# The first unit's gates written out in one fixed order, and its first chunk taken from angles to keys and queries by groups of four heads

## The chip, the cores and the metric

The kernel runs on one core of a Trainium2 chip. The metric is the device time of one execution in microseconds (us). The kernel before took 724.6 us in the median of four runs (722.34 to 727.52).

## The reference, cut to what matters

Two blocks follow each other. The first is a gated linear recurrence over 768 time steps for 4 batches of 8 heads with 48 channels each:

```python
mag = np.sqrt(a_re * a_re + a_im * a_im)
scale = np.minimum(mag, 0.999) / (mag + 1e-06)
a_re_n, a_im_n = (a_re * scale, a_im * scale)
for t in range(S):
    new_re = ar * S_re - ai * S_im          # ar, ai: the gate of step t
    new_im = ar * S_im + ai * S_re
    kv = np.einsum('bhd,bhe->bhde', k[:, :, t], v[:, :, t])
    S_re, S_im = (new_re + kv, new_im)
    y[:, :, t] = np.einsum('bhd,bhde->bhe', q[:, :, t], S_re)
```

The second is a feed-forward block on the 3072 rows of 384 values that come out: `h = x @ w_in` (384 to 2048), `g = h * erf(softplus(h))`, `g @ w_out`. The two weights arrive as 64-bit floats and are narrowed to 32 bits on the chip.

## The kernel before, in words

**The algorithm.** A product of complex gates is the exponential of a sum of logarithms and of a sum of angles. So the recurrence becomes attention in chunks: `g_tan` (L873) makes a_im/a_re from Ln and Exp; `g_mag` (L863) and `g_log` (L883) make the logarithm `lr` of the magnitude; `g_turn` (L891) takes the arctangent; `g_total` (L923) and `g_angle` (L895) sum logarithms and angles along time by a matmul with a triangle; `g_decay` (L927) takes Exp of plus and minus the sum (tile `pr`), and `g_sin` (L915) sine and cosine of the angle (tile `CS`). In `chunk` (L954), `prep` multiplies keys and queries by `pr` (L950, tiles `kr`, `qr`) and by `CS` (L965, tiles `kt`, `qt`); `cols` transposes four heads at a time on TensorE (L973) and copies them out of PSUM (L976); `scores` (L980), `state` (L991) and `xT` (L1010) are the attention itself. `ff_in` (L1043, tile `hps`), `softplus`, `erf_times_h` and `ff_out_7`/`ff_out_8` are the feed-forward block.

**The tiling.** The rows are cut into 12 units of 256 rows, each of two chunks (`c0`, `c1`) of 128. The first matmul of `ff_in` of a unit needs `xT` of both its chunks.

**What sets the order.** The program is traced once, without loops on the chip. A list scheduler then fixes the order on every engine: it goes by the order of tracing and lets an instruction go ahead of earlier ones that, by its own model, are not ready. `in_order` (L710) chains the ScalarE instructions that need a function table, so that tables are not swapped more often than written; `T["hold"]` ties the first VectorE step of a weight's narrowing behind another instruction. The first chunk's gates are traced by hand (L1225 to L1262). All after it is a list `plan` of pairs (time, step), sorted by the numbers in `WHEN` (L47), in which one unit of time is about one unit of rows. `warm` (L1206) issues matmuls whose results nobody reads; each appears as two in the trace.

**Function tables.** Ln and Exp are in one table, Arctan and Sin in a second, Gelu in a third. Every change of table is an `ACT_TABLE_LOAD` on ScalarE (L707).

**Narrowing the weights.** `narrow` (L747) works on 16 pieces of 768 KB: a DMA (`raw`, L763), one ScalarE multiplication (L769) and three VectorE operations (L772, L776, L782).

Of the kernel before, what the change touches and what calls it, by code (L numbers as in the profile page):

```python
# [10 lines left out]
FP = mybir.dt.float32  # L11
# [24 lines left out]
def weave(*streams):  # L36
# [5 lines left out]
    for _, _, _, step in sorted(order, key=lambda e: e[:3]):  # L42
# [4 lines left out]
WHEN = {'qact': 2,  # L47
 'a00': [0.385, 0.377, 0.389, 0.465, 0.427, 0.308, 0.569, 0.485, 0.567, 0.63],
 'a01': [0.526, 0.422, 0.611, 0.633, 0.649, 0.542, 0.659, 0.66, 0.67, 0.681],
 'n': [0.676, 0.782, 0.769, 0.929, 1.105, 1.183, 1.312, 1.472, 1.61, 1.914, 1.96, 2.143, 2.151, 2.632, 2.395],  # L50
 'g1': [0.657, 0.707, 0.747, 0.758, 0.79, 0.797, 0.829],
 'att': {1: [[0.931, 1.297], 1.089], 2: [[1.716, 2.126], 1.029], 3: [[3.038, 3.627], 1.205]},
 'gate': {2: [1.242, 1.289, 1.402, 1.421, 1.453, 1.472, 1.392], 3: [1.516, 1.614, 1.92, 2.114, 2.598, 2.232, 2.18]},
 'hps': {0: [[0.767, 0.876], [1.01, 1.426]],
         1: [[1.788, 2.017], [2.366, 2.708]],
         2: [[3.136, 3.262], [3.538, 3.85]],
         11: [[11.97, 12.305], [12.367, 12.72]]},
 'act': {0: [2.6, 2.924],
         1: [3.335, 3.7],
         2: [4.134, 4.386],  # L60
         3: [4.9, 5.2],
         4: [5.752, 6.098],
         10: [11.679, 12.029],
         11: [12.456, 12.886]},
 'ops': {0: [3.02, 3.377, 3.703],
         1: [4.059, 4.696, 4.846],
         2: [4.454, 4.8, 4.886],
         3: [5.38, 5.6, 6.213],
         10: [12.145, 12.41, 13.01],
         11: [13.169, 13.36, 14.059]},  # L70
 'T': 5.1,
 'gr': [-1.569, -1.419, -1.119, -0.953, -0.478, -0.129, -1.279],
 'st': [0.014, 0.03, 0.059, 0.09, 0.12, 0.15, 0.2, 0.25, 0.28, 0.388],
 'hr': [1.113, 1.509, 1.573, 1.938],
 'ar': [1.565, 1.947],
# [3 lines left out]
 'ag': [5.424, 6.296, 7.239, 8.239, 9.239, 10.239, 11.21],  # L79
# [4 lines left out]
 'qone': 0}  # L84


WARM = (12, 9, 8, 8, 13, 5)
# [511 lines left out]
def quotient_path(  # L599
# [19 lines left out]
    nc = tc.nc  # L619
    B, H, S, D = q.shape  # L620
# [44 lines left out]
    nc.vector.memset(cold, 0.0)  # L665
    ones = const.tile([P, 1], FP, name="ones")
    nc.vector.memset(ones, 1.0)
    half_pi = const.tile([P, 1], FP, name="half_pi")
    nc.vector.memset(half_pi, 0.5 * math.pi)
    turns = const.tile([P, P], FP, name="turns")  # L670
    nc.vector.tensor_scalar(out=turns, in0=triu, scalar1=1.0 / TAU, scalar2=None, op0=OP.mult)
# [3 lines left out]
    for t, x in ((off, 0.0), (large, 0.0), (zeros, 1.0)):  # L675
        nc.vector.memset(t, x)
# [11 lines left out]
    for t in vbuf:  # L688
        nc.vector.memset(t[:, :, :, D:D + GAP], 0.0)
    for t in sbuf:  # L690
        nc.vector.memset(t[:, :, D:D + GAP], 0.0)
# [8 lines left out]
    def act(func, **kw):  # L700
        sets = [nm for nm, fs in TABLES.items() if func in fs]
        if not sets:
            nc.scalar.activation(func=func, **kw)
            return
        if T.get("table") != sets[0]:
            T["table"] = sets[0]
            in_order(nc.scalar.preload_act_table_set(sets[0]))  # L707
        in_order(nc.scalar.activation(func=func, **kw))  # L708
# [38 lines left out]
    def narrow(i, dst, src, home):  # L747
# [6 lines left out]
        def seek(words, i):  # L754
            hi = words.bitcast(FP).rearrange("p (n w) -> p n w", w=2)[:, :, 1]
            nc.vector.tensor_reduce(out=zeros[:, i:i + 1], in_=hi, axis=mybir.AxisListType.X, op=OP.min,  # L756
                                    apply_absolute_value=True)
# [7 lines left out]
        def begin():  # L765
# [3 lines left out]
            ins = nc.scalar.mul(out=lo, in_=lo, mul=2.0**-29)  # L769
            if i < 3:  # L770
                in_order(ins)
            ins = nc.vector.tensor_scalar(out=a, in0=hi, scalar1=0x07FFFFFF, scalar2=3, op0=OP.bitwise_and,  # L772
                                          op1=OP.logical_shift_left)
            if "hold" in T:
                tc.add_manual_dep(ins.ins, T["hold"].ins.name, order, reason="place among others")
            nc.vector.scalar_tensor_tensor(out=a, in0=hi, scalar=0xC0000000, in1=a, op0=OP.bitwise_and,  # L776
                                           op1=OP.bitwise_or)
            T["parts", i] = a, lo

        def end():  # L780
            a, lo = T["parts", i]
            nc.vector.tensor_tensor(out=dst.bitcast(U32), in0=a, in1=lo, op=OP.add)  # L782

        def use():
            begin()
            end()
# [9 lines left out]
        if i < 14:  # L796
            return get, use, again, look, begin, end
# [10 lines left out]
        return get, use, again, look, begin, end  # L808
# [25 lines left out]
    def sums_of_weights(r0, n):  # L834
# [8 lines left out]
        for o, x, y in ((T1, B12, B11), (T2, B22, T1), (T4, B21, T2), (B12, B22, B12)):  # L843
            nc.vector.tensor_tensor(out=o, in0=x, in1=y, op=OP.subtract)
# [18 lines left out]
    def g_mag(u, cc=ALL):  # L863
# [4 lines left out]
        i = u * C + cc[0]  # L868
        act(out=s, in_=ar, func=AF.Square, accum_out=large[:, i:i + 1])
        act(out=y, in_=ai, func=AF.Square)  # L870
        nc.vector.tensor_tensor(out=s, in0=s, in1=y, op=OP.add)

    def g_tan(u, cc=ALL):  # L873
# [4 lines left out]
        nc.vector.tensor_tensor(out=th, in0=th, in1=ai, op=OP.mult)  # L878
        i = u * C + cc[0]
        nc.vector.tensor_reduce(out=off[:, i:i + 1], in_=th, axis=mybir.AxisListType.XY, op=OP.max,  # L880
                                apply_absolute_value=True)

    def g_log(u, cc=ALL):  # L883
# [4 lines left out]
        nc.vector.tensor_scalar(out=s, in0=s, scalar1=0.5, scalar2=math.log(CAP), op0=OP.mult, op1=OP.min)  # L888
        T["logs"] = nc.vector.tensor_tensor(out=g_("lr", u, cc), in0=s, in1=y, op=OP.subtract)
# [5 lines left out]
    def g_angle(u, c):  # L895
# [4 lines left out]
        if goes_on:  # L900
            prev = T["F", u][:, c - 1, :] if c > 0 else T["F", u - 1][:, C - 1, :]
            if not on_pe:
                row = T["s", u][0:1, c, :]
                nc.sync.dma_start(out=row, in_=prev[P - 1:P, :])
                nc.vector.scalar_tensor_tensor(out=th[0:1, :], in0=row, scalar=TAU, in1=th[0:1, :],
# [6 lines left out]
        nc.vector.tensor_scalar(out=F, in0=ps, scalar1=MAGIC, scalar2=MAGIC, op0=OP.add, op1=OP.subtract)  # L912
        nc.vector.tensor_tensor(out=F, in0=ps, in1=F, op=OP.subtract)

    def g_sin(u, cc=ALL):  # L915
# [5 lines left out]
        act(out=CS[:, :, 1, :], in_=F, func=AF.Sin, scale=TAU)  # L921

# [24 lines left out]
    def scaled(nm, e, u, c):  # L947

        a = att1.tile([P, H, D], FP, tag="part", name=nm + "r", bufs=2)
        nc.vector.tensor_tensor(out=a, in0=T[nm, u][:, c], op=OP.mult,  # L950
# [3 lines left out]
    def chunk(u, c):  # L954
# [3 lines left out]
        st = {}  # L958

        def prep(nm, e):  # L960
            def f():
# [3 lines left out]
                T["hold"] = nc.vector.tensor_tensor(out=t, in0=a.unsqueeze(2).to_broadcast([P, H, 2, D]), in1=cs, op=OP.mult)  # L965
# [3 lines left out]
        def cols(nm, g):  # L969
            def f():  # L970
# [5 lines left out]
                (nc.scalar.copy if nm == "k" or u < WHEN["qact"] or g < WHEN["qone"] else nc.vector.tensor_copy)(out=t[0:D2], in_=ps[0:D2])  # L976
# [3 lines left out]
        def scores(g):  # L980
            def f():
# [5 lines left out]
                nc.vector.tensor_tensor(out=A, in0=ps, in1=triu.unsqueeze(1).to_broadcast([P, HG, P]), op=OP.mult)  # L987
# [3 lines left out]
        def state():  # L991
# [10 lines left out]
            else:  # L1002
                t = att1.tile([P, H, D], FP, tag="part", name="Skv", bufs=2)
                for e in range(2):
                    nc.vector.tensor_tensor(out=t[0:D2, e::2, :], in0=kv[0:D2, e::2, :], in1=side(T["S"][0:D2], e), op=OP.add)  # L1005
            for e in range(2):
                nc.vector.tensor_tensor(out=side(ns[0:D2], e), in0=t[0:D2, e::2, :], in1=w[:, e::2, :], op=OP.mult)
            st["S"] = ns

        def xT():  # L1010
# [26 lines left out]
            nc.scalar.copy(out=T["xT", u][:, :, c * P:(c + 1) * P], in_=ps)  # L1037
# [5 lines left out]
    def ff_in(u, sl):  # L1043
        def two(i):
            def f():
# [9 lines left out]
                nc.scalar.copy(out=T["h", u, sl][:, i:i + 2, :], in_=ps)  # L1055
# [15 lines left out]
    def erf_times_h(u, sl):  # L1071
# [3 lines left out]
        def part(i):  # L1075
            def f():
# [4 lines left out]
                nc.vector.tensor_tensor(out=z, in0=z, in1=y, op=OP.mult)  # L1081
                nc.vector.scalar_tensor_tensor(out=y, in0=z, scalar=-2.0, in1=y, op0=OP.add, op1=OP.mult)  # L1082
                nc.vector.tensor_tensor(out=e, in0=e, in1=y, op=OP.mult)  # L1083
                nc.vector.scalar_tensor_tensor(out=h, in0=e, scalar=1.0 / RT2, in1=h, op0=OP.add, op1=OP.mult)  # L1084
# [294 lines left out]
```

## Time and profile before

| | us |
|---|---|
| median of four runs | 724.6 |
| the profiled execution | 721.8 |
| its span, from first to last instruction | 720.0 |
| TensorE busy in the span | 704.0 |
| VectorE busy | 577.2 |
| ScalarE busy | 568.4 |
| 77 table loads on ScalarE, 1.283 us each | 98.8 |
| mean granted TensorE clock, as a share of full speed | 0.998 |

In the lines of the timeline and of the chain the first number is the start in us from the beginning of the span and the second the duration. The chain of waits goes back from the last instruction: each step is followed to what released it, or to the instruction before it on its engine. PE is TensorE's matmuls, PEld its weight loads, DVE VectorE, ACT ScalarE, SP the engine that issues most DMAs. An instruction on ACT or DVE can begin before the one ahead of it has fully ended, so that starts follow each other closer than the durations say.

### The profile page before, as it was taken

To read this page: it belongs to the slowest core of one execution; us is meant where nothing else is said; L and a number is where in the kernel's file an instruction comes from. 1 tells how busy PE (TensorE), PEld (TensorE's weight loads), DVE (VectorE), ACT (ScalarE), POOL (GpSimd) and SP (SyncE) were. 2 spreads that over 40 slices of the span, in tenths; PEclk is the share of its full clock that TensorE was granted. 3 is DMA by queue.
4 is the path that set the end of the run, shared out by engine and by line. 5 is a ranking of instruction groups with operands and counts; after the bars stand their busy time and mean duration, and the time that the engine had idled before them with its cause. 6 is when DMAs were issued, how large, how long until landed. Compare 5 with 4: busy or idle time off the path is not lost.

```text
span 720.0 us, 12616 instructions
## 1 busy us (share of the span) xinstructions
PE 704.0 (98%) x5050; PEld 602.7 (84%) x5050; DVE 577.2 (80%) x1003; ACT 568.4 (79%) x749; POOL 1.1 (0%) x8
## 2 busy tenths in 40 slices
PE   9899999999999999999999999999999999999996
PEld 8778888766777678898998998889898899899985
DVE  5878996777599789979899889797798877876563
ACT  7978949978988998799788688887688487556760
POOL 0000000000000000000000000000000000000000
PEclk9999999999999999999999999999999999999999
DMA  9985784021303211613322423323330400200000
GB/s 215 228 191 120 199 211 94 1 45 34 56 0 57 55 45 25 146 31 76 89 56 55 112 56 68 105 50 67 100 99 23 132 1 23 89 1 23 0 24 27
DMA packets 156012, 54.50 MB, mean 76 GB/s; under 512 B 142612, under 2 KB 145704, under 8 KB 155944
## 3 DMA queue, kind: packets, MB, share of 16 engines
q1 hardware_dynamic: 153864, 53.22, 31.6%
q8 instruction: 41, 0.67, 0.4%
q10 hardware_dynamic: 2080, 0.39, 0.4%
q14 instruction: 27, 0.22, 0.1%
HBM read 48.82 MB, written 4.75 MB: 74 GB/s over the span
## 4 chain that ended last, share of the span: by engine, by line
PE 52%; ACT 24%; DVE 17%; DMA 4%; issue 2%; SPq 0%; ACTq 0%
PE hps L1053 20%; PE ops L1151 14%; ACT z L708 5%; ACT L707 5%; ACT yy L708 4%; PE tr L973 3%; PE y L1033 3%; PE sc L984 3%; DVE z L1081 3%; DVE yy L1082 3%; DVE e L1083 2%; PE kv L996 2%; DVE h L1084 2%; PE ops L1113 2%; DMA again<-in_moe_w_out_dram 2%
## 5 line engine op out<-in xcount | busy, mean ns | idle before, releaser
L1053 PE MATMUL hps<-xT,w_in_sb 128*128 128x256 f32 x1152 | 270.7, 381 | 1.0 <-ACT xT L1037 0.7
L1053 PEld LDWEIGHTS hps<-xT,w_in_sb 128*128 128x128 f32 x1152 | 212.5, 190 | 33.1 <-issue 2.6
L707 ACT ACT_TABLE_LOAD x77 | 98.8, 1283 | 3.3 <-issue 2.1
L1055 ACT COPY h<-hps 128x512 f32<-128x512 f32 x96 | 55.3, 580 | 44.8 <-PE hps L1053 42.1
L708 ACT ACTIVATE e<-z 128x512 f32<-128x512 f32 x96 | 57.3, 626 | 37.1 <-DVE h L1084 36.7
L1081 DVE TENSOR_TENSOR z<-z,yy 128x512 f32<-128x512 f32 x96 | 62.6, 683 | 29.4 <-ACT e L708 28.9
L1113 PE MATMUL ops<-w_out_sb,h 128*128 128x384 f32 x224 | 76.6, 488 | 0.4 <-DVE h L1084 0.4
L1151 PE MATMUL ops<-w_out_sb,h 128*128 128x192 f32 x384 | 70.5, 326 | 0.0
L1151 PEld LDWEIGHTS ops<-w_out_sb,h 128*128 128x128 f32 x384 | 63.6, 190 | 1.4
L1113 PEld LDWEIGHTS ops<-w_out_sb,h 128*128 128x128 f32 x224 | 41.5, 190 | 26.5 <-DVE h L1084 1.2
L1082 DVE SCALAR_TENSOR_TENSOR yy<-z,yy 128x512 f32<-128x512 f32 x96 | 62.4, 682 | 0.1
L1083 DVE TENSOR_TENSOR e<-e,yy 128x512 f32<-128x512 f32 x96 | 62.4, 681 | 0.1
L1084 DVE SCALAR_TENSOR_TENSOR h<-e,h 128x512 f32<-128x512 f32 x96 | 62.4, 680 | 0.1
L708 ACT ACTIVATE z<-h 128x2048 f32<-128x2048 f32 x24 | 45.9, 1913 | 9.7 <-DVE seen L756 4.9
L984 PEld LDWEIGHTS sc<-qT,kT 96*128 96x128 f32 x384 | 47.9, 191 | 5.7 <-DVE qT L976 3.0
L984 PE MATMUL sc<-qT,kT 96*128 96x128 f32 x384 | 50.9, 278 | 1.7 <-DVE qT L976 1.3
L1033 PE MATMUL y<-A,v 128*32 128x128 f32 x768 | 47.6, 278 | 0.6 <-DVE Skv L1005 0.5
L1151 PE MATMUL ops<-T,S 128*128 128x192 f32 x256 | 47.4, 327 | 0.0
L708 ACT ACTIVATE yy<-z 128x2048 f32<-128x2048 f32 x24 | 45.9, 1913 | 0.4
L708 ACT ACTIVATE z<-z 128x2048 f32<-128x2048 f32 x24 | 45.9, 1913 | 0.3
L708 ACT ACTIVATE yy<-yy 128x2048 f32<-128x2048 f32 x24 | 45.9, 1913 | 0.3
L1151 PEld LDWEIGHTS ops<-T,S 128*128 128x128 f32 x256 | 42.3, 190 | 2.1 <-DVE S L1165 0.3
(101 smaller groups left out, 1063.5 us busy)
## 6 DMA issues: line engine op xcount, KB each, us to landing
raw<-in_moe_w_in_dram SPq DMA_DIRECT2D x8, 768.0 KB, 9.4
raw<-in_moe_w_out_dram SPq DMA_DIRECT2D x8, 768.0 KB
again<-in_moe_w_in_dram SPq DMA_DIRECT2D x8, 768.0 KB, 6.3
ar<-in_a_re_dram SPq DMA_DIRECT2D x24, 192.0 KB, 3.1
k<-in_k_dram SPq DMA_DIRECT2D x24, 192.0 KB, 4.1
q<-in_q_dram SPq DMA_DIRECT2D x24, 192.0 KB, 3.6
v<-in_v_dram SPq DMA_DIRECT2D x48, 96.0 KB, 3.3
out_dram<-o SPq DMA_DIRECT2D x24, 192.0 KB, 1.9
```

What stands on the lines that cost most here:

```text
L707: in_order(nc.scalar.preload_act_table_set(sets[0]))
L708: in_order(nc.scalar.activation(func=func, **kw))
L984: nc.tensor.matmul(out=ps[:, j, :], lhsT=st["k", g][0:D2, j, :], rhs=st["q", g][0:D2, j, :], start=True, stop=True)
L1033: nc.tensor.matmul(out=ps[b * QUAD:(b + 1) * QUAD, i, :], lhsT=lhsT, rhs=rhs, start=start, stop=stop)
L1053: nc.tensor.matmul(out=ps[:, e, :], lhsT=w_in_sb[:, kd, f0:f0 + P], rhs=T["xT", u][:, kd, :], start=(kd == 0), stop=(kd == KD - 1))
L1055: nc.scalar.copy(out=T["h", u, sl][:, i:i + 2, :], in_=ps)
L1081: nc.vector.tensor_tensor(out=z, in0=z, in1=y, op=OP.mult)
L1082: nc.vector.scalar_tensor_tensor(out=y, in0=z, scalar=-2.0, in1=y, op0=OP.add, op1=OP.mult)
L1083: nc.vector.tensor_tensor(out=e, in0=e, in1=y, op=OP.mult)
L1084: nc.vector.scalar_tensor_tensor(out=h, in0=e, scalar=1.0 / RT2, in1=h, op0=OP.add, op1=OP.mult)
L1113: nc.tensor.matmul(out=ps, lhsT=lhsT, rhs=w_out_sb[:, i, :], start=i == HALF, stop=i == KF - 1)
L1151: ins = nc.tensor.matmul(out=ps, lhsT=a(sl)[:, i], rhs=b(sl, i), start=sl == 0 and i == 0, stop=sl == NSL - 1 and i == HALF - 1)
```

## The change

**A fixed order.** A class `InOrder` wraps VectorE and ScalarE. While it is on, every instruction is tied behind the one traced before it on its engine. It is on from the first gate instruction of unit 0 to `g_decay(0, 1)`; elsewhere the wrapper does nothing.

**Another order.** Before, both chunks' tangents and magnitudes came first, then the logarithm of c0, Arctan of both, the decay of c0 and the sines of both, and the logarithm of c1 last: the table of Ln and Exp is loaded three times and that of Arctan and Sin twice. Now the logarithm of c0, the tangents of c0 and c1 and the decay of c0 come ahead of the first Arctan, and the magnitude and logarithm of c1 after the last sine: two loads and one. The first step of the narrowing of the first weight piece is split: its VectorE steps (`high`) go ahead of the decay, its ScalarE step and its sum (`low`, `join`) behind all gates.

**By groups.** For chunk 0 of unit 0, `by_heads` does the angle, its sine and cosine and the last multiplication of keys and queries in two halves of four heads, with the absolute value taken on VectorE.

**The rest.** The search for the largest tangent, `g_off`, is a step of its own. The copies of transposed queries out of PSUM go to VectorE for the first chunk and for units from 3 on (before: from 2 on), so that unit 2's are on ScalarE now. `warm` multiplies the zero tile `cold` only, and its counts are others. Many numbers in `WHEN` differ, most by little; unit 1's gates (`g1`) come 0.045 later.

```diff
-WHEN = {'qact': 2,
- 'a00': [0.385, 0.377, 0.389, 0.465, 0.427, 0.308, 0.569, 0.485, 0.567, 0.63],
- 'a01': [0.526, 0.422, 0.611, 0.633, 0.649, 0.542, 0.659, 0.66, 0.67, 0.681],
- 'g1': [0.657, 0.707, 0.747, 0.758, 0.79, 0.797, 0.829],
+WHEN = {'qact': 3,
+ 'a00': [0.385, 0.699, 0.3, 0.32, 0.31, 0.33, 0.569, 0.34, 0.35, 0.63],
+ 'a01': [0.526, 0.422, 0.611, 0.637, 0.649, 0.542, 0.659, 0.66, 0.67, 0.681],
+ 'g1': [0.702, 0.752, 0.792, 0.802, 0.835, 0.842, 0.873],
...
-WARM = (12, 9, 8, 8, 13, 5)
+WARM = (16, 0, 16, 2, 3, 4)
+class InOrder:
+    def __init__(self, tc, engine):
+        self.tc, self.engine, self.on = tc, engine, False
+    def __getattr__(self, name):
+        emit = getattr(self.engine, name)
+        if not self.on:
+            return emit
+        return lambda *args, **kw: self.tc.keep_in_program_order(emit(*args, **kw))
...
+    def by_heads():
+        F = g_("F", 0, (0, 1))[:, 0, :]
+        CS = T["CS", 0] = gat.tile([P, C, 2, DM], FP, tag="CS", name="CS")
+        of = lambda t, g: t[..., g * HG * D:(g + 1) * HG * D]
+        got = {nm: att1.tile([P, H, 2, D], FP, tag=nm + "t", name=nm + "t") for nm in ("k", "q")}
+        def angle(g):
+            ps = ps_a.tile([P, HG * D], FP, tag="a", name="sum")
+            nc.tensor.matmul(out=ps, lhsT=turns, rhs=of(T["th", 0][:, 0, :], g), start=True, stop=True)
+            vector.tensor_scalar(out=of(F, g), in0=ps, scalar1=MAGIC, scalar2=MAGIC, op0=OP.add, op1=OP.subtract)
+            vector.tensor_tensor(out=of(F, g), in0=ps, in1=of(F, g), op=OP.subtract)
+            vector.scalar_tensor_tensor(out=of(CS[:, 0, 0], g), in0=of(F, g), scalar=-1.0, in1=of(F, g), op0=OP.mult, op1=OP.max)
+        def sin(g):
+            act(out=of(CS[:, 0, 1], g), in_=of(F, g), func=AF.Sin, scale=TAU)
+            act(out=of(CS[:, 0, 0], g), in_=of(CS[:, 0, 0], g), func=AF.Sin, scale=-TAU, bias=half_pi)
+        def prep(nm, g):
+            cs = of(CS[:, 0], g).rearrange("p u (h d) -> p h u d", d=D)
+            hh = slice(g * HG, (g + 1) * HG)
+            ins = vector.tensor_tensor(out=got[nm][:, hh], in0=T["r", nm, 0, 0][:, hh].unsqueeze(2).to_broadcast([P, HG, 2, D]),
+                                       in1=cs, op=OP.mult)
+            T["hold"] = ins
+        return angle, sin, prep, got
...
-                (nc.scalar.copy if nm == "k" or u < WHEN["qact"] or g < WHEN["qone"] else nc.vector.tensor_copy)(out=t[0:D2], in_=ps[0:D2])
+                (vector.tensor_copy if nm == "q" and ((u, c) == (0, 0) or u >= WHEN["qact"] and g >= WHEN["qone"]) else scalar.copy)(out=t[0:D2], in_=ps[0:D2])
...
+    angle, sin, prep, T["first"] = by_heads()
     first = chunk(0, 0)
-    for c in range(C):
-        g_tan(0, one[c])
-        g_mag(0, one[c])
-        warm(WARM[1 + c], T["th", 0][:, c])
+    vector.on = scalar.on = True
+    T["table"] = "natural_log_exp_and_others"
+    in_order(scalar.preload_act_table_set(T["table"]))
+    g_mag(0, c0)
     g_log(0, c0)
+    g_tan(0, c0)
+    warm(WARM[1], cold)
+    g_off(0, c0)
     g_total(0, 0)
-    for cc in one:
-        g_turn(0, cc)
-    T["hold"] = T["logs"]
-    wt[0][4]()
-    g_angle(0, 0)
+    g_tan(0, c1)
+    g_off(0, c1)
+    warm(WARM[2], cold)
+    _, _, _, _, high, low, join = wt[0]
+    high()
     g_decay(0, 0)
-    for nm, e in (("k", 1), ("q", 0)):
-        T["r", nm, 0, 0] = scaled(nm, e, 0, 0)
-    wt[0][5]()
+    T["r", "k", 0, 0] = scaled("k", 1, 0, 0)
+    g_turn(0, c0)
+    angle(0)
+    angle(1)
+    warm(WARM[3], cold)
+    g_turn(0, c1)
+    sin(0)
+    prep("k", 0)
+    sin(1)
+    T["r", "q", 0, 0] = scaled("q", 0, 0, 0)
+    prep("k", 1)
+    g_angle(0, 1)
+    warm(WARM[4], cold)
+    prep("q", 0)
+    prep("q", 1)
+    g_mag(0, c1)
+    g_sin(0, c1)
+    g_log(0, c1)
+    g_total(0, 1)
+    g_decay(0, 1)
+    vector.on = scalar.on = False
+    low()
+    join()
     wt[2][0]()
-    warm(WARM[3], T["th", 0][:, 1])
-    g_sin(0, c0)
-    for f in first[:2]:
-        f()
-    g_angle(0, 1)
-    warm(WARM[4], T["th", 0][:, 1])
-    g_sin(0, c1)
     wt[1][1]()
     load_gates(1)
     for j in (3, 4, 5):
         wt[j][0]()
-    g_log(0, c1)
-    g_total(0, 1)
-    g_decay(0, 1)
```

## The prediction

> **What bounds the kernel now.** I read the page's busy times, then windows, the chain of waits and the timeline of the first 55 us.
>
> ```profile
> PE 704.0 (98%) x5050; PEld 602.7 (84%) x5050; DVE 577.2 (80%) x1003; ACT 568.4 (79%) x749; POOL 1.1 (0%) x8
> ```
>
> TensorE is busy for all but 16 us, so the time is its work plus what it loses. Busy isn't useful, though: the groups show 24 + 86 warm matmuls, 5.5 + 10.5 us, all before 22.2. Windows (busy us of PE, PEld, DVE, ACT, POOL, then the granted clock):
>
> ```profile
> 20.00:25.00 5.00, 3.95 (x29) 3.26 (x30) 3.23 (x5) 4.97 (x10) 0.00 (x0) 1.00 0.98 180
> 25.00:30.00 5.00, 4.95 (x50) 4.20 (x49) 4.09 (x7) 5.00 (x15) 0.00 (x0) 1.00 1.02 356
> 60.00:80.00 20.00, 20.00 (x172) 16.70 (x172) 19.61 (x30) 19.29 (x30) 0.00 (x0) 1.00 0.79 193
> 80.00:100.00 20.00, 18.79 (x175) 16.81 (x178) 19.63 (x33) 15.58 (x24) 0.00 (x0) 1.00 0.76 185
> ```
>
> Until 25 ScalarE is the full engine, and TensorE idles or warms. From 25 TensorE is full, so whatever brings useful matmuls forward shortens the end, as long as VectorE, which is full too from 60 to 100, keeps up. The chain (start, duration, what) names ScalarE up to the first scores:
>
> ```profile
> 13.06 1.28 ACT L707
> 14.34 0.01 issue
> 14.35 0.96 ACT pr L708 x3
> ...
> 15.74 1.28 ACT L707
> ...
> 20.38 1.28 ACT L707
> 21.66 0.01 issue
> 21.67 0.52 ACT s L708
> 22.19 0.47 ACT qT L976
> 22.66 0.42 ACT y L708
> 23.09 0.47 ACT kT L976
> 23.56 0.42 ACT y L708
> 23.98 0.48 ACT qT L976
> 24.46 0.04 issue
> 24.51 0.49 PE sc L984 x2
> ```
>
> Keys and queries of c0 are rotated by 19.92 (`qt` starts at 18.97 and takes 0.95), but their copies out of PSUM stand behind a table load and among c1's logarithms: first scores 24.51. Four timeline lines are my milestones: keys of c1, first useful `hps`, keys of unit 1, their transposes.
>
> ```profile
> 29.04 0.94 DVE L965 TENSOR_TENSOR kt<-kr,CS 128x768 f32<-128x768 f32 x1
> ```
> ```profile
> 40.05 3.19 PE L1053 MATMUL hps<-xT,w_in_sb 128*128 128x256 f32 x14
> ```
> ```profile
> 49.59 0.95 DVE L965 TENSOR_TENSOR kt<-kr,CS 128x768 f32<-128x768 f32 x1
> ```
> ```profile
> 53.50 1.04 PE L973 MATMUL tr<-ident,kt 128*96 128x128 f32 x8
> ```
>
> **Step 1: to the decay of c0, in the fixed order.** Rows: 128x384 costs 0.52 on ACT (start to start 0.41, but 0.55 where one reads the last one's result), 0.55 on DVE (0.47). The first Square starts when `ar` lands, 4.53 as now; the second ends at 5.6; DVE adds until 6.16. ACT, which now fills that wait with other work, stands idle 0.6. Ln, Exp, Ln of the magnitude start at 6.19, 6.75, 7.31; `lr` is done at 8.42 (10.65 now). The tangents follow at 7.72, 8.27, 8.69, 9.24. The sum of c0 is on PE from 8.45 to 9.33, so the two Exps of `pr` start at 9.67 behind the tangents and ACT is free at 10.52 (15.20 now). `high` stands ahead of `kr` on DVE and waits for the first weight piece; that was read at 10.57 without a wait, and comes to its turn at 10.93. `kr` is done at 12.93. Moving the weight's ACT step (0.91) and sum (0.96) behind the gates frees that much here; they fall into ACT's and DVE's waits after 22. The DMAs of `wrow` stand in SP's queue behind c1's values, whose issues end at 14.7, so they aren't earlier; unit 1's gate loads, issued from 18.18, now wait for c1's Squares, which end at 16.8: 1.4 us of cover.
>
> **Step 2: angles by halves.** Table load 10.52 to 11.80, Arctan of c0 until 12.33. 32 warm matmuls start behind the sum at 9.10 and take 32 x 0.112 = 3.6, so angle 0 starts at 12.7 and ends at 13.3. DVE has a row for half width, 0.35 (L1172); three dependent steps end at 13.66, 14.04, 14.42, the second half's at 15.46. ACT has no 128x192 row: between 0.26 (half of 0.52) and 0.52, I take 0.36 from the slope between 0.52 at 384 and 0.83 at 768; either end moves nothing, because DVE's order sets the steps after it. Sines of half 0 end at 14.9, of half 1 at 15.95. `prep` of k: 15.93 and 16.87; then `F` of c1 (0.55 twice) until 17.93; q: 18.40 and 18.87. Against 19.92 that is only 1.05 earlier. The two halves cost four extra DVE starts of about 0.15 and the absolute value 2 x 0.35 on DVE instead of 0.52 on ACT, all counted here.
>
> **Step 3: scores of c0.** `kT` is copied by ACT by 18.1, while c1's angle is still on DVE. `qT` goes to DVE (0.68 against 0.58 on ACT), 19.2 to 19.85 and to 20.5. First scores: 19.9, **4.6 earlier**. Here the two dropped table loads count: c1's logarithm no longer stands in the middle.
>
> *Page against row:* the load takes 1.283 and the next ACT instruction starts 0.01 later. The Trainium skill, "ScalarE: Activation LUTs", section "What ACT_TABLE_LOAD costs", adds a drain of about 1.38 to each change of table; by it two loads fewer would save 5.3, by the row 2.57. The measurement decides; no sum here uses 5.3.
>
> **Step 4: keys of c1.** Sines of c1 end at 19.57, table load until 20.85, logarithm until 22.48, `lr` 23.07, sum 24.0, `pr` 24.9; `qt` at 26.1 and `kt` at 27.55, **2.4 earlier** than 29.98.
>
> **Step 5: to the first `hps`.** PE's work from first scores on, by the chain's rows: scores 2 x 1.85, state 2 x 1.32, three sums of 0.65, transposes of c1 4 x 0.44, `y` 1.70 and 2.18, together 13.93. Before, 40.05 - 24.51 = 15.54, so 1.61 was lost. After: until `kt` of c1 PE has 6.40 of work for 7.70 us, 1.30 lost, and the same 1.61 on the copies and masks. First `hps`, with the same work done: 19.9 + 13.93 + 2.91 = 36.74, **3.3 earlier**. Bounds: only the 1.30 lost, 4.9; the copies and masks lose 2 more because narrowing and unit 1's gates come between, 1.3.
>
> **Step 6: the rest.** Unit 2's four `qT` copies leave DVE (4 x 0.68) for ACT (4 x 0.58), between 80 and 110, where DVE is full and PE loses 1.2 from 80 to 100. Worth 0 to 1.2, I take 0.7. The other numbers of `WHEN` shuffle a PE that is full; no row prices them: 0, with 1.5 either way for the range. The start's warm work goes from 110 to 82 instructions, and is worth nothing while the clock stays up. A first-speed warm matmul takes 421 ns against 275 later, the windows show 1.00 until 717 and 0.50 after, and the last matmul ended at 714.46: an idle stretch of 2.5 us is enough. My longest gap is 1.1, before the queries; were the clock lost there, some 3 us of work would take 3 more.
>
> *Page against row:* "TensorE: Matmul & The Clock Gate", Part 1, says that an idle window of about 3.4 us halves the clock, the windows running free of the program, and warns against the gaps that fewer warm matmuls leave. The row's 2.5 is stricter; by neither does 1.1 lose the clock.
>
> **The sum.** The profiled execution took 721.8 (span 720.0, 1.8 around it): 721.8 - 3.3 - 0.7 = 717.8. The median of the runs lies 724.6 / 721.8 = 1.0039 above it: **720.6**. The forecast's own bounds, 1.3 to 6.1 earlier, are 718.5 to 723.3.
>
> **The rivals.**
> A, *the gain is handed back at units 1 and 2.* DVE is 98% busy from 60 to 100 and its work isn't less by more than 2; if it, not PE, sets the pace there, PE meets it again. For: ACT copies of `xT` and DVE's `Skv` hold PE up at 80 to 86. Against: PE loses nothing from 60 to 80. Price: 3.3 of the gain; 724.
>
> B, *slower: unit 1's keys come late.* Its gates stand 0.045 later in the plan, and PE takes the transposes in order. Now `kt` ends at 50.54 for a transpose at 53.50, 3.0 to spare; with `hps` 3.3 earlier, they're due at 50.2. If unit 1's gates slip behind three groups of `ff_in` (12 matmuls, 2.59 each: 7.8), `kt` ends at 58.3, PE stands 8.1, and 4.0 of gain leaves a loss of 4.1: 728.7. It decides once `kt` ends later than 54.2. Against: ACT has 4 us less to do before 40 (two loads, 2.57; one Abs, 0.52; two copies, 1.16), and the scheduler lets ready gates go ahead.
>
> C, *the change doesn't do what it says:* fixed order makes ACT wait (for `F` of c1, for the sum) with c1's logarithm behind it, `kt` of c1 stays near 29.4, and PE makes nothing of early scores: 0.6 earlier, 724.
>
> D, *more:* PE isn't starved for c1 and loses nothing: 19.9 + 13.93 = 33.8, 6.2 earlier, with step 6 some 7: 717.6.
>
> **How the numbers follow.** Forecast 0.60, A 0.17, C 0.08, B 0.09, D 0.06. A measurement can tell about 0.5%, 3.6 us, from no change; that line is 721.0, inside the forecast's own range, and I put 0.42 of its 0.60 below it. Faster: 0.42 + 0.06 = 0.48; same: 0.18 + 0.17 + 0.08 = 0.43; slower: 0.09. The range leaves out B and part of D: 717.5 to 725.0.
>
> **What the profile after would show.** Right: three table loads before 40 us, one of them for Arctan and Sin, instead of five up to 21; first `sc` near 19.9, `kt` of c1 near 27.5, first `hps` near 36.7, transposes of unit 1 near 50. Wrong: an `hps` early and an unchanged end (A), PE idle before unit 1's `tr` (B), `kt` of c1 past 29 (C), or a granted clock of 0.50 before 25.

## The result and the profile after

| | before | after |
|---|---|---|
| median, us (59 and 38 runs) | 723.97 | 725.8 |
| profiled execution / its span, us | 721.8 / 720.0 | 725.2 / 723.5 |
| last matmul ends, us | 714.46 | 715.98 |
| table loads in the trace | 77 | 93 |
| weight pieces 0 and 1 joined (`w_in_sb` starts), us | 13.3, 21.5 | 27.2, 31.2 |

The ratio is **1.0034**, 95% interval 1.0025 to 1.0043 (the two medians alone give 1.0025): the kernel became some 2.5 us slower, where 4.0 us, 0.55%, faster was forecast. The granted clock differs from execution to execution, but it isn't the loss: with a mean of 0.997 or more the kernel before takes 722.8 us (103 of the 137 executions beside the experiments) and the changed one 725.2 (21 of 40). All ratios below are to the kernel before, run on the same chip.

The page's busy times first:

```profile
PE 701.0 (97%) x5024; PEld 600.7 (83%) x5024; DVE 579.0 (80%) x1007; ACT 590.4 (82%) x768; POOL 1.1 (0%) x8
```

TensorE has 3.0 less to show, and ScalarE 22 more. The same windows as before (busy us of PE, PEld, DVE, ACT, POOL, then the clock):

```profile
20.00:25.00 5.00, 4.14 (x30) 3.53 (x31) 2.76 (x6) 3.03 (x6) 0.00 (x0) 1.00 0.97 171
25.00:30.00 5.00, 4.12 (x64) 3.61 (x63) 4.62 (x8) 5.00 (x12) 0.00 (x0) 1.00 0.88 286
60.00:80.00 20.00, 19.64 (x156) 15.89 (x154) 18.98 (x31) 17.90 (x28) 0.00 (x0) 1.00 0.69 159
80.00:100.00 20.00, 18.67 (x173) 16.92 (x174) 17.26 (x30) 17.86 (x27) 0.00 (x0) 1.00 0.80 203
```

ScalarE, full from 20 to 25 before (4.97 of 5.00), is idle for 2 of these 5 us, and full in the next five. The chain of waits shows the start itself (start, duration, what):

```profile
13.00 0.34 PE sum L958 x2
13.37 0.37 DVE F L100
...
18.02 0.93 DVE qt L100 x2
18.95 0.47 DVE s L100
19.42 0.61 DVE qT L1028
20.08 0.66 PE tr L1025 x4
20.76 0.70 DVE qT L1028
21.50 2.05 PE sc L1036 x16
23.55 0.45 PE unread L1262 x4
24.00 0.83 PE sum L977 x2
24.85 0.96 ACT pr L100 x3
25.82 1.66 ACT raw L796 x2
```

No table load stands in this stretch any more; the angles and rotations come as worked out, and the scores begin at 21.50 (24.51 before). The last line is the price: both multiplications of weight pieces 0 and 1 come after the decay of c1. The joins of these two pieces on VectorE, before and after:

```profile
13.31 0.95 DVE L782 CUSTOM_DVE_ANT_0 w_in_sb<-raw,word 128x1536 uint16<-128x1536 uint16 x1
21.52 0.96 DVE L782 CUSTOM_DVE_ANT_0 w_in_sb<-raw,word 128x1536 uint16<-128x1536 uint16 x1
```
```profile
27.19 0.95 DVE L802 CUSTOM_DVE_ANT_0 w_in_sb<-raw,word 128x1536 uint16<-128x1536 uint16 x1
31.16 0.96 DVE L802 CUSTOM_DVE_ANT_0 w_in_sb<-raw,word 128x1536 uint16<-128x1536 uint16 x1 [0.28 <-ACT kT L1028]
```

The milestones in the timeline (keys of c1, `hps`, keys of unit 1, their transposes):

```profile
28.06 0.95 DVE L1017 TENSOR_TENSOR kt<-kr,CS 128x768 f32<-128x768 f32 x1
```
```profile
38.36 1.13 PE L1105 MATMUL hps<-xT,w_in_sb 128*128 128x256 f32 x4 [0.21 <-ACT xT L1089]
40.60 2.43 PE L1105 MATMUL hps<-xT,w_in_sb 128*128 128x256 f32 x10 [1.11 <-DVE w_in_sb L802]
```
```profile
50.94 0.96 DVE L1017 TENSOR_TENSOR kt<-kr,CS 128x768 f32<-128x768 f32 x1 [1.65 <-ACT CS L725]
```
```profile
54.41 1.04 PE L1025 MATMUL tr<-ident,kt 128*96 128x128 f32 x8
```

The first `hps` is 1.7 early, and after four matmuls TensorE waits for a weight piece. The keys of c1 are 1.0 early, unit 1's are 1.35 **late**. TensorE's waits from 36 to 80 (engine and line, waited for: us, times, longest); before, there is none in this stretch:

```profile
PE hps L1105 <- DVE w_in_sb L802: 1.8, 2, 1.1
```

The two waits end with the third and the fourth join, begun at 39.59 and 43.32 (37.38 and 41.06 in run 6 below, where pieces 0 and 1 are early). Pieces 0 and 1 themselves are there by 32.1; it is the work behind them on ScalarE and VectorE that comes late.

The second trouble lies far from the start. ScalarE's timeline, one stretch of a later unit (start, duration):

```profile
468.70 1.28 ACT L724 ACT_TABLE_LOAD   x1
470.00 0.63 ACT L725 ACTIVATE e<-z 128x512 f32<-128x512 f32 x1
470.64 1.28 ACT L724 ACT_TABLE_LOAD   x1
471.94 0.87 ACT L725 ACTIVATE pr<-sum 128x384 f32<-128x384 f32 x2
472.70 0.21 ACT L725 ACTIVATION_READ_ACCUMULATOR pr<-sum 128x1 f32 x1
472.79 0.88 ACT L725 ACTIVATE pr<-sum 128x384 f32<-128x384 f32 x2
473.53 0.23 ACT L725 ACTIVATION_READ_ACCUMULATOR pr<-sum 128x1 f32 x1
473.76 1.28 ACT L724 ACT_TABLE_LOAD   x1
475.06 0.63 ACT L725 ACTIVATE e<-z 128x512 f32<-128x512 f32 x1
```

The decay (`pr`) of the next unit falls between two parts `e` of the feed-forward that need another table, and costs two loads more. Before, it came at 453.86, ahead of steps of its own table. Of the changed numbers only 'ar' does this (1.565 to 1.472, the due time of the first slab's part in later units): the changed kernel has 75 loads with 'ar' put back, and the kernel before has 95 with it alone.

### The profile page after: what moved, and what is told of

Same layout as the page of the kernel before. It is cut to its first block, busy times and chain, and to the rows that moved or that the text cites. A ratio compares the mean times of both kernels' runs of the same rounds, so it can differ in the third digit from the quotient of the medians.

```text
span 723.5 us, 12579 instructions
## 1 busy us (share of the span) xinstructions
PE 701.0 (97%) x5024; PEld 600.7 (83%) x5024; DVE 579.0 (80%) x1007; ACT 590.4 (82%) x768; POOL 1.1 (0%) x8
## 3 DMA queue, kind: packets, MB, share of 16 engines
HBM read 48.82 MB, written 4.75 MB: 74 GB/s over the span
## 4 chain that ended last, share of the span: by engine, by line
PE 43%; ACT 33%; DVE 18%; issue 3%; DMA 2%; ACTq 0%; DVEq 0%
PE hps L1105 15%; PE ops L1203 10%; ACT L724 7%; ACT yy L725 6%; ACT z L725 6%; PE ops L1165 4%; PE tr L1025 3%; DVE z L1133 3%; DVE yy L1134 2%; PE sc L1036 2%; ACT e L725 2%; DVE e L1135 2%; PE y L1085 2%; DVE h L1136 2%; ACT th L725 2%
```

## The experiments

The runs are numbered from 1 to 17 in the order in which they stand here; brackets hold the 95% interval. Going by these intervals, the ratios of two runs can be told apart from about 0.2%, 1.4 us, on.

**1 to 4: which part.** Two theories stood against each other: T, the table loads of 'ar' (the "softplus number" of the expectations) are the loss, and S, the new start is. The changed kernel with 'ar' back:

```diff
- 'ar': [1.472, 1.947],
+ 'ar': [1.565, 1.947],
```

> The kernel after with one number of WHEN as before: 'ar' 1.565 instead of 1.472 (softplus of the first slab of units 5 to 9 at its old place). Theory T: the 13 more table loads that the trace after shows (90 against 77, most between 360 and 600 us) are the loss; they go, PE loses some 2.7 us less between 350 and 550, and the ratio to before is 0.9995 or lower. Theory S: the start itself is the loss (PE lost 25.7 us in the first 80 against 23.5), the loads stand on an engine with time to spare; the ratio stays at 1.003.

Measured: 1.0016 [1.0003, 1.0029], between the two forecasts. (The 90 loads named there are those of one line; three more stand under the line of the fixed order, 93 in all.) The changed code with all numbers of before, except those that place the new start:

```diff
-WHEN = <the changed numbers>
+WHEN = <the numbers before, with 'a00', 'a01' and 'c1g' as changed>
```

> The new start alone: all of after's code with the first chunk's numbers a00 and a01, every other number of WHEN as before. T: ratio 0.996 to 0.999, the start's own gain, handed back only in part. S: ratio 1.002 to 1.004, with PE waiting for weight pieces and unit 1's keys before 80 us as in the trace after.

Measured: 1.0064 [1.0046, 1.0082]. The code and start of before with all the other changed numbers:

```diff
-WHEN = <the numbers before>
+WHEN = <the changed numbers, with 'a00' and 'a01' as before>
```

> The old start with all other numbers of after's WHEN. T: ratio 1.003 to 1.005, over 90 table loads. S: ratio 0.999 to 1.001.

Measured: 0.9995 [0.9983, 1.0007]. The kernel before with 'ar' alone:

```diff
- 'ar': [1.565, 1.947],
+ 'ar': [1.472, 1.947],
```

> The kernel before with 'ar' 1.472 alone. T: ratio 1.003 to 1.004 and over 90 table loads, the price of that one number. S: ratio 0.999 to 1.001, although the loads are there.

Measured: 1.0045 [1.0029, 1.0060]. Run 3 is in S's range, run 4 a little above T's, run 2 well above S's. So neither theory holds alone: both parts lose, and the rest of the numbers gives something back. 'ar' costs 0.18% as a difference of two ratios in the changed kernel and 0.45% in the one before. The second figure holds some clock as well: in run 4's profile the granted clock is 0.50 from 180.0 to 186.9, far from the added loads. Among executions with a mean clock of 0.997 or more 'ar' costs 0.22 and 0.31% (in run 4 these are only three).

**5 to 8: what is wrong with the start.** Theory V: the fixed order leaves ScalarE waiting early and pushes its volume, the weight pieces above all, behind. Rival C (another than the prediction's C): the chain of chunk 0 is late, since its second key copy comes at 21.38, behind c1's sines. Runs 5 to 7 have 'ar' back, so their base is run 1, 1.0016. Second key copy early:

```diff
- 'a00': [0.385, 0.699, 0.3, 0.32, 0.31, ...
+ 'a00': [0.385, 0.699, 0.3, 0.305, 0.31, ...
```

> The changed kernel with the softplus number back at 1.565, and one more number: the second half of chunk 0's keys is transposed and copied before the first half of its queries (0.305 in the place of 0.32), so that both key copies stand ahead of chunk 1's sines on ScalarE. The base for it is the changed kernel with the softplus number alone put back (ratio 1.0016 to the kernel before). Theory C, the chain: the start is late because chunk 0's second key copy came at 21.38, behind the sines; then the first scores come near 20, chunk 1's keys some 1.5 earlier than 28.1, and the ratio falls to 0.9995 or lower. Theory V, the volume: ScalarE and VectorE have lost their room to the waits of the fixed order, and what is narrowed late stays late; then the first scores are early and the ratio stays between 1.000 and 1.002.

Measured: 1.0014 [0.9999, 1.0029]. Its timeline of TensorE, then of VectorE:

```profile
20.05 2.05 PE L1037 MATMUL sc<-qT,kT 96*128 96x128 f32 x16 [0.36 <-DVE qT L1029]
```
```profile
27.11 0.95 DVE L803 CUSTOM_DVE_ANT_0 w_in_sb<-raw,word 128x1536 uint16<-128x1536 uint16 x1
28.91 0.95 DVE L1018 TENSOR_TENSOR kt<-kr,CS 128x768 f32<-128x768 f32 x1
```

The scores now begin 4.46 before their old place, nearly as predicted, and no time clear of noise comes of it. The weight piece stays where run 1 has it (27.09), and the keys come later rather than earlier: c1's by 0.96 (27.95 in run 1), unit 1's by 0.97 (51.80 for 50.83). C, which asked for 0.9995 or less and earlier keys, falls. (Five of the 12 executions have a mean clock of 0.995 or less, none of run 1's; at 0.997 or more run 5 has 1.0002 and run 1 1.0012, so a gain of some 0.7 us may hide behind the clock.) Weight pieces 0 and 1 into the waits:

```diff
     g_turn(0, c1)
+    low()
     sin(0)
...
     prep("q", 1)
+    join()
+    wt[1][4]()
     g_mag(0, c1)
     g_sin(0, c1)
     g_log(0, c1)
+    wt[1][5]()
     g_total(0, 1)
     g_decay(0, 1)
+    wt[1][6]()
     vector.on = scalar.on = False
-    low()
-    join()
     wt[2][0]()
-    wt[1][1]()
```

(`wt[1][4]`, `[5]`, `[6]` are piece 1's `high`, `low` and `join`.)

> The changed kernel with the softplus number back, and weight pieces 0 and 1 narrowed inside the fixed order, in the places in which ScalarE waits: piece 0's multiplication ahead of the first sine (a wait of 1.3 us), piece 1's ahead of chunk 1's decay (a wait of 1.9 us), their joins on VectorE behind the queries and behind chunk 1's decay. Theory V expects about 1.9 us of ScalarE's work to move out of the stretch from 25 to 40, unit 1's gates that much earlier, and a ratio of 0.998 to 1.000 where the base has 1.0016. Theory C expects nothing of it: 1.001 to 1.003, since the second key copy is as late as before and the first scores still come near 21.5.

Measured: **0.9970** [0.9956, 0.9984], faster than the kernel before, 0.46% under its base, and faster than V's own range. Unit 1's keys come at 48.82 (50.83 in run 1), and TensorE waits for no weight. The joins in its timeline of VectorE, and TensorE's window from 38 to 80, which holds 39.66 in the changed kernel:

```profile
18.89 0.95 DVE L101 CUSTOM_DVE_ANT_0 w_in_sb<-raw,word 128x1536 uint16<-128x1536 uint16 x1
25.14 0.95 DVE L101 CUSTOM_DVE_ANT_0 w_in_sb<-raw,word 128x1536 uint16<-128x1536 uint16 x1
```
```profile
38.00:80.00 42.00, 41.68 (x279) 33.80 (x278) 33.30 (x54) 36.50 (x61) 0.00 (x0) 1.00 0.74 173
```

The fixed order off (everything else as in run 1):

```diff
-    vector.on = scalar.on = True
```

> The changed kernel with the softplus number back and the fixed order off: the same instructions, but the scheduler may place those of the start on ScalarE and VectorE where it likes, except those that were pinned before the change too. Theory V: the waits of the fixed order (about 5 us of ScalarE before 34) are filled again, and the ratio is at or below the base's 1.0016, between 0.998 and 1.0016. Theory C: the order on ScalarE decides little against that on the transposes, so the same within 0.15%. If the fixed order is what keeps tables from being loaded more often, the ratio is above 1.003 and the page shows more table loads before 40.

Measured: 1.0075 [1.0057, 1.0092]; no theory had it, V's forecast fails as well. There are no more table loads than in its base. The scheduler put both chunks' sums of squares and the weight's first step, which waits for its DMA until 9.12, ahead of `lr` on VectorE, and TensorE stood still. Its timeline of TensorE, and three windows of it (busy, then the granted clock):

```profile
11.57 1.62 PE L978 MATMUL sum<-lr,triu 128*128 128x384 f32 x2 [5.26 <-DVE lr L916]
12.97 5.96 PE L1263 MATMUL unread<-cold 128*128 128x128 f32 x32
```
```profile
10.00:11.00 1.00, 0.00 (x0) 0.90 1.43 180
11.00:12.00 1.00, 0.43 (x1) 0.50 0.97 206
...
18.00:19.00 1.00, 1.00 (x11) 1.00 1.04 375
```

The 32 warm matmuls take 5.96, most of them at half clock, where they take 3.73 in its base, and the scores begin at 26.63 instead of 21.39. So the fixed order by itself isn't the fault: without it, this order of tracing is 0.59%, 4.3 us, slower. The old start with the other changed numbers, 'ar' excepted:

```diff
-WHEN = <the numbers before>
+WHEN = <the changed numbers, with 'a00', 'a01' and 'ar' as before>
```

> The kernel before with all of the changed kernel's other numbers except the softplus number, which stays at 1.565; 77 table loads as in the kernel before. If the softplus number costs the 0.18 to 0.45% that two runs gave it, and the numbers behind it bring something by themselves, 0.995 to 0.998, faster than both kernels; then the new start is the part that loses. If the other numbers bring nothing without the new start, 0.9985 to 1.001.

Measured: **0.9972** [0.9959, 0.9984]. That is the sum in three terms: the numbers without 'ar' -0.28%; the new start on top of them 1.0016 - 0.9972 = +0.44%; 'ar' +0.18%. The terms depend on the order in which they are taken: the new start costs 0.39% on top of all numbers (run 3 to the changed kernel) and 0.64% with the old ones (run 2).

**9 to 12: the lateness by itself, and the numbers.** Unit 2's query copies alone, in the kernel before:

```diff
-WHEN = {'qact': 2,
+WHEN = {'qact': 3,
```

> The kernel before with one number of the change alone: the query copies of unit 2 go back from VectorE to ScalarE ('qact' 3 in the place of 2). Theory Q: these copies on VectorE make the scores of unit 2 wait (1.3 us of TensorE at 165 in the trace before, gone in every trace with 'qact' 3, where the shift against the kernel before drops by 2 us between 116 and 167); then this number alone is what makes the other numbers pay, ratio 0.9965 to 0.9985. Rival, the prediction's own term: ScalarE takes on four copies and loses some 0.7 us by them, 1.000 to 1.001, and what the other numbers bring comes from the others.

Measured: 1.0027 [1.0012, 1.0043]. The old wait of `sc` for `qT` (it ends at 177.67; the expectation has 165) is gone, and TensorE's waits from 80 to 202 show what stands in its place (0.7 before):

```profile
PE tr L974 <- DVE kt L966: 3.3, 1, 3.3
```

Theory Q falls. The wait ends at 133.38, and from 134.0 to 137.4 the granted clock is 0.50. Seven of this run's 12 executions have a mean clock of 0.995 or less, and one has 0.997 or more. Run 6 with unit 1's gates as early as before:

```diff
- 'g1': [0.702, 0.752, 0.792, 0.802, 0.835, 0.842, 0.873],
+ 'g1': [0.657, 0.707, 0.747, 0.758, 0.79, 0.797, 0.829],
```

> The run with weight pieces 0 and 1 narrowed in the waits of the fixed order (ratio 0.997), and unit 1's gates due as early as in the kernel before (0.657 to 0.829 in the place of 0.702 to 0.873). There unit 0's outputs are 3.5 and 2.0 us early and unit 1's only 0.3, since unit 1's angles come late (the sines wait 1.1 and 2.0 us for them). If it is the due times that hold them, unit 1's outputs come 1 to 2 us earlier and the ratio is 0.994 to 0.996. If ScalarE's volume up to 40 holds them, the ratio stays at 0.997 or rises, since the gates then push the weights back: 0.9965 to 0.9985.

Measured: 0.9999 [0.9979, 1.0020], slower than run 6 rather than faster. Unit 1's keys come at 48.95 (48.82 in run 6): the due time wasn't what held them. The fourth weight piece is joined at 45.16 instead of 41.06, pushed back as the volume's theory has it; the interval is wide and reaches that theory's 0.9965 to 0.9985. The late weights alone, in run 8:

```diff
-    wt[0][4]()
...
-    wt[0][5]()
-    wt[2][0]()
...
-    wt[1][1]()
-    load_gates(1)
...
     g_decay(0, 1)
+    wt[0][4]()
+    wt[0][5]()
+    wt[2][0]()
+    wt[1][1]()
+    load_gates(1)
```

(The loads of pieces 3 to 5 stay behind `load_gates(1)`. Unit 1's gate loads move with the weights in the text, but are issued only 0.1 to 1.0 later.)

> The old start with the changed kernel's other numbers except the softplus number (ratio 0.9972), and weight pieces 0 and 1 narrowed behind chunk 1's decay, where the changed kernel has them. No fixed order here: ScalarE stays full. If it is the late weights that cost the new start its gain (1.8 us of TensorE waiting for them in the trace after), the same wait appears here, and the ratio is 0.999 to 1.001. If it is the waits of the fixed order alone, the gates move up into the place of the weights and nothing is lost: 0.9965 to 0.998.

Measured: 1.0011 [0.9996, 1.0027], 0.39% above run 8. TensorE's waits from 36 to 80, of which run 8 has none:

```profile
PE hps L1054 <- DVE w_in_sb L783: 2.2, 2, 1.7
```

The joins are at 26.3 and 30.9 here, the first scores at 22.93 and so 1.46 **earlier** than in run 8 (24.39), unit 1's keys at 52.52 instead of 47.85. No fixed order, no halves: the late weights alone give the changed start's loss. Run 10 with the second key copy early too (the edit of run 5):

> The run before the last (weights in the waits, unit 1's gates as early as before), and chunk 0's second key copy ahead of chunk 1's sines too. Alone on the changed kernel that copy brought nothing (1.0014 beside 1.0016) while the weights were late. If it was hidden behind the weights, it now shows: 0.2 to 1 us below the run without it. If unit 0's start is no longer on the path, the two agree within 0.15%.

Measured: 0.9995 [0.9981, 1.0009], as run 10 within 0.04%. The times alone couldn't show a gain of 0.2 to 1 us, but the trace agrees: the first scores come 1.2 earlier (20.49 for 21.66), the first `hps` doesn't (38.90 for 38.82). Unit 0's start isn't on the path here.

**13 to 17: which numbers pay.** The pair of query copies and unit 2's and 3's gates, then the gates alone, in the kernel before:

```diff
-WHEN = {'qact': 2,
+WHEN = {'qact': 3,
- 'gate': {2: [1.242, 1.289, 1.402, 1.421, 1.453, 1.472, 1.392], 3: [1.516, ...
+ 'gate': {2: [1.212, 1.259, 1.372, 1.391, 1.423, 1.442, 1.362], 3: [1.508, ...
```

> The kernel before with two of the numbers: the query copies of unit 2 on ScalarE ('qact' 3) and unit 2's and 3's gates due 0.03 and 0.008 earlier ('gate'). The first alone gave 1.0027: it took away the 1.3 us for which the scores of unit 2 waited, and put 3.3 us in their place for which unit 2's first keys are waited for. Theory G: the earlier gates take those 3.3 us away, and the pair is what the other numbers bring: 0.996 to 0.998, as all of them together on the old start (0.9972). Rival: the pair gives 1.000 or more, and a third number is needed.

> The kernel before with unit 2's and 3's gates due earlier alone ('gate'), the query copies of unit 2 left on VectorE. Theory G: the wait for unit 2's queries stays, and ScalarE has its room already, so 0.999 to 1.001. Rival: the gates alone bring it, 0.996 to 0.998, and the copies bring nothing.

Measured: 0.9999 [0.9984, 1.0014] and 1.0035 [1.0023, 1.0048]. Theory G falls, and the gates alone fit neither forecast; their trace no longer has the wait for unit 2's queries, though the copies stay on VectorE. Run 6 with unit 1's angles earlier on TensorE:

```diff
- 'g1': [0.702, 0.752, 0.792, 0.802, 0.835, 0.842, 0.873],
+ 'g1': [0.702, 0.752, 0.792, 0.789, 0.82, 0.842, 0.873],
```

> The run with weight pieces 0 and 1 narrowed in the waits of the fixed order (ratio 0.997), with only the angles of unit 1 placed earlier among TensorE's work (0.789 and 0.82 in the place of 0.802 and 0.835), its gates' work on ScalarE left where it is. There unit 0's outputs were 3.5 and 2.0 us early and unit 1's only 0.3, and its sines waited 1.1 and 2.0 us for the angles. If the place of the angles on TensorE is what holds unit 1, 0.994 to 0.996, faster than every other kernel here. If TensorE has work at that time anyway (41.7 of 42 us busy between 38 and 80), the same 0.997 within 0.1%.

Measured: 0.9984 [0.9968, 1.0000]: not faster than run 6. The sines' waits for the angles are gone, but unit 1's decays come at 44.88 instead of 39.63 and its keys at 51.70 instead of 48.82, so the place of the angles alone isn't what holds unit 1. Among executions with a mean clock of 0.997 or more the two runs are closer still, at 0.9971 and 0.9978. The pair with an earlier up-projection (`ff_in`), and all numbers of run 8 without it. The edit is the whole of 'hps', so that units 2 and 11 move with unit 1:

```diff
-         1: [[1.788, 2.017], [2.366, 2.708]],
-         2: [[3.136, 3.262], [3.538, 3.85]],
-         11: [[11.97, 12.305], [12.367, 12.72]]},
+         1: [[1.778, 2.017], [2.342, 2.684]],
+         2: [[3.136, 3.262], [3.538, 3.868]],
+         11: [[11.97, 12.371], [12.438, 12.72]]},
```

> The kernel before with three of the numbers: the query copies of unit 2 on ScalarE, unit 2's and 3's gates earlier, and the up-projection of unit 1 earlier ('hps', its second slab 2.342 to 2.684 in the place of 2.366 to 2.708). The first two gave 0.9999, with 1.8 us of waiting for unit 2's first keys and 0.9 for a copy of unit 1's up-projection left between 120 and 140. If the up-projection is the third number, these waits fall to 1.0 and nothing, and the ratio to 0.997 to 0.998. If it is spread over the others ('ops', 'T', 'st', 'n', 'g1'), 0.999 to 1.000.

> The old start with all of the changed kernel's other numbers except the softplus number (0.9972), and without the earlier up-projection of unit 1 ('hps' as before). If that one carries the gain, 0.999 to 1.001; if it is spread over the others, 0.997 to 0.998.

Measured: 0.9995 [0.9981, 1.0009] and 1.0016 [1.0002, 1.0031]. No number carries the gain. Copies and gates lose 0.27% and 0.35% alone and nothing together; the up-projection brings little to the pair, and 0.44% where all others are in place. How the rest divides is open, and so is why the gates alone cost 0.35%: their profiled trace shows no loss of that size, and the clock isn't it (0.38% among executions at 0.997 or more).

## Why the prediction was wrong, step by step

**Step 1** was right in its times (the decay of c0 at 9.65 for 9.67, `kr` at 12.39 to 12.94 for 12.93) and wrong in one sentence, the dearest of all: that the weight's ScalarE step and sum "fall into ACT's and DVE's waits after 22". After 22 ScalarE's only long wait (1.93, before the decay of c1) lies inside the fixed order, and they were traced behind it. They came at 25.71, when ScalarE is full (5.00 of 5.00), with unit 1's gates and the next weight pieces behind them. The cost was set at nothing; run 6 and run 11, from both sides, put it at 0.46 and 0.39%, about 3 us.

**Step 2** held to 0.1: the queries are rotated at 18.95 for 18.87. The 128x192 step on ScalarE took 0.36, the value taken, and 0.46 where it has a bias.

**Step 3** was 1.6 out, at 21.50 for 19.9. TensorE takes the second key transpose behind the first query's, and its copy (21.38) stands behind c1's sines and a table load. The pool for these tiles in PSUM has two buffers; with one held so long, the second query transpose (20.08) and the scores each wait for a query copy to free the other. With the order turned round in run 5 the scores came at 20.05, without a gain in time that is clear of noise.

**Step 4** had the decay right (24.85 for 24.9), but the join of piece 0 stands ahead of `kt` on VectorE: 29.01 for 27.55. The join is 0.87 of that; the rest was in the sum, since `kt` behind a `qt` that starts at 26.32 (26.1 was worked out) can't end before 28.14.

**Step 5** is where the sum broke. 3.3 was taken for "the same work done"; the first `hps` came at 38.36, 1.7 early, and not with the same work, for only one of unit 1's two sums was done. And the milestone itself was no measure. The first `hps` of run 6, then of run 8, which take the same time (0.9970 and 0.9972, last matmuls at 712.79 and 712.70):

```profile
37.97 2.86 PE L1106 MATMUL hps<-xT,w_in_sb 128*128 128x256 f32 x12
```
```profile
39.93 3.19 PE L1054 MATMUL hps<-xT,w_in_sb 128*128 128x256 f32 x14
```

By 80 us both have the same matmuls behind them, 96 of `hps`, 64 of `sc` and 64 of `kv`; no wait of TensorE names the place where run 6's lead goes. The changed kernel has 96, 56 and 48 by then. The scores up to 80 in run 6, run 8 and the changed kernel:

```profile
L1037 PE MATMUL sc<-qT,kT 96*128 96x128 f32 x64 | 8.8, 282 | 1.3 <-ACT qT L1029 0.5 <-ACT kT L1029 0.5 <-DVE qT L1029 0.3
L985 PE MATMUL sc<-qT,kT 96*128 96x128 f32 x64 | 8.8, 280 | 0.3 <-ACT qT L977 0.3
L1036 PE MATMUL sc<-qT,kT 96*128 96x128 f32 x56 | 7.3, 280 | 1.4 <-DVE qT L1028 0.8 <-ACT qT L1028 0.6
```

The term was 3.3; a lead of 2.0 at the same milestone was worth nothing between runs 6 and 8.

**Step 6** priced the other numbers at 0, 1.5 either way, the query copies at a gain of 0.7. Alone the copies lose 0.27%, about 2.0 us (run 9); its profile has 3.4 us at half clock. The numbers give -0.28% without 'ar', and 'ar' takes 0.18 to 0.45% back, 1.3 to 3.3. Its 18 loads (95 for 77) at 1.283 are 23 us of ScalarE; ScalarE's 24.6 more from 350 to 640 in run 4 agree. They could have been counted ahead. The drain of 1.38 that the Trainium skill adds to a load ("ScalarE: Activation LUTs", "What ACT_TABLE_LOAD costs") isn't seen here either: `e` starts at 470.00, 0.02 after the load's end.

**The rivals.** A has the right form, an early `hps` handed back; but its reason, VectorE from 60 to 100, is not it: VectorE is less full there than before (18.98 and 17.26 of 20 for 19.61 and 19.63). B's way was entered, keys of unit 1 at 51.90 instead of 50.54, but not its point of 54.2. C's keys stayed late, 29.01, but not for its reason: c1's logarithm began at 20.95, where 20.85 was worked out, and the join of piece 0 came between. Three table loads before 40 us came true. The clock held in the profiled execution, but the argument for it doesn't: the longest gap there is 1.31, not 1.1, and run 15, with the same gap, lost the clock (last section).

## What to carry to other kernels

An early first milestone was worth nothing by itself here: ask of each instruction that a new order puts later where it will stand, and whether that engine has room there, before asking what comes earlier. In a start that one engine fills, put the moved work into the waits that the new order makes. Count the function-table loads whenever a due time moves on ScalarE, and try numbers tuned together as a set, since two that each lose can be part of a gain.

## What the runs showed of the hardware

An idle TensorE lost its clock after some 4.5 us: in run 7 the last warm matmul ended at 6.30, the granted clock fell to 0.50 at about 10.8 (0.90 over the slice from 10) and was back at about 17.6, six microseconds after work began again. At the end of the kernel before, 2.5 us were enough, and 2.1 at the end of run 6; the changed kernel and run 8 took 4.5 and 4.7. The Trainium skill, "TensorE: Matmul & The Clock Gate", Part 1, names a free-running window of about 3.4 us for either change: 4.5 and 4.7 lie between one window and two, 2.1 and 2.5 don't fit. (It warns against idle gaps; of fewer warm matmuls, which the prediction adds, it says nothing.)

It can also be lost without such a stretch. In run 15 no gap before the fall is longer than 1.31 us, but TensorE is busy for only 2.90 of the 5 us from 18 to 23 (busy, then the granted clock):

```profile
18.00:23.00 5.00, 2.90 (x21) 2.21 (x21) 4.96 (x10) 4.03 (x7) 0.00 (x0) 1.00 1.00 215
24.00:25.00 1.00, 1.00 (x7) 1.00 (x6) 0.61 (x2) 0.79 (x1) 0.00 (x0) 0.50 0.62 114
```

In run 4 a wait of 1.34 that ends at 178.43 stands ahead of 6.8 us at half clock; the kernel before has the same wait, and its profiled execution kept the clock. So executions of one kernel differ: 14 of the changed kernel's 40 have a mean clock of 0.995 or less and take 728.1 us, 21 have 0.997 or more and take 725.2; of the 137 of the kernel before beside the experiments these are 24 at 725.3 and 103 at 722.8. Where the changed kernel's 14 lost it, no trace here shows.

The time from the last matmul to the end of the span is between 5.5 and 7.5 us, in one profile each: 5.5 before, 7.5 after, 7.3 in run 14 with the old start, 5.6 in run 15 with the new one. It doesn't go with the start, so that of the 3.5 between the two profiled spans only 1.5 is at TensorE.
